# Seven block products for eight in the second half of a first MLP product, with a shorter weight conversion and Silu on ScalarE

## The chip, the cores and the metric

The kernel runs on one core of one Trainium2 chip. Its engines work side by side, each through a queue of its own in order: TensorE (PE in the profile; its weight loads are PEld), VectorE (DVE), ScalarE (ACT), GpSimd (POOL) and SyncE (SP), which here issues the transfers. They wait for one another by semaphores. The metric is device time in microseconds (us), as a median of several runs.

## The reference

Attention over 4 batches and 12 heads (448 tokens, 64 wide) with normed q and k feeds two MLP layers over 1792 tokens, 768 wide, hidden 2048:

```python
q_n, k_n = (rmsnorm(q, g_q), rmsnorm(k, g_k))
attn = softmax(scale * q_n @ k_n.T)                  # with the row's maximum taken off
x = (attn @ v) as 1792 x 768
h = x @ w_in;   x1 = (h * (1 / (1 + exp(-h)))) @ w_out        # first layer
h = x1 @ w2_in; r = maximum(h, 0); out = (r * r) @ w2_out     # second layer
```

The weights of both layers arrive as 64-bit floats; the kernel reads them as pairs of 32-bit words.

## The kernel before

**Numbers.** Each matmul operand is held in two parts: a high part (a cast to TensorE's 32-bit format) and a low part (the rest). A product is three matmuls: high x high, low x high, high x low. `split` makes the parts of activations, `parts` those of weights (`w_hi` by ScalarE or VectorE, `w_lo` by VectorE or GpSimd, L515 to L524).

**Weights.** `words` loads 64-bit weights into a buffer `raw` (a ring of three), and builds 32-bit floats from their words: an absolute value on ScalarE (L876), a clamp (L880), a shift (L884), the sign (L890) and the low bits (L896) on VectorE. It stores the result in device memory for later loads. The first layer's weights are converted in its first half (16 blocks of `w_in`, 24 of `w_out`); the 32 blocks of the second layer's weights are converted ahead of time, into a buffer `V`, during the first layer, by the list `BEFORE` and the function `ahead`.

**First layer.** Tokens lie in four batches of 448; the first half works on batches 0 and 1, the second on 2 and 3. A half has four quarters of four hidden blocks of 128. In a quarter, `up` makes, for each block and batch, 18 matmuls (six channel blocks by three) into a bank of the ring `t` (three banks), then a tanh on ScalarE (L989) and a multiply on VectorE (L994) give twice the Silu in `g`, which is split into `gg` (`g_hi`, `g_lo`). Then the out-projection goes into the ring `s` (four banks), and is added to `part` (L1043) with a factor 0.5; the last quarter's sums are stored as `y`.

**Second layer.** It treats its inputs as 2 x 2 blocks: two hidden blocks by two channel halves, and two channel halves by two batches. `combine` forms sums of input blocks (B11, T2, T3, T4, B21, T1, B22), `weights` sums of weight blocks (S1 to S4, L1161), and seven products (L1193, nine matmuls each) with sums out of the banks (`plus`, L1209, on VectorE) replace eight.

**Order.** The order on all engines is found when the program is built: `Plan` holds every step with a duration, runs them forward by due time, works the due times backward from the end, and keeps the best of several rounds. The attention's steps have fixed nominal times. Buffers come from rings, and a step that claims a buffer waits for the users of the one before.

## Time and profile before

| | us |
|---|---|
| median of three timed runs | 1199.5 |
| lowest and highest of them | 1197.34 and 1202.25 |
| the profiled execution | 1194.88 |
| its span | 1193.0 |

The page gives for each engine its busy time and share of the span: TensorE 98%, weight loads 88%, VectorE 77%, ScalarE 46%, GpSimd 21%. Attention fills the time up to about 272 us, the first layer the time to about 745 us, the second the rest. The granted clock of TensorE is full in all of the forty slices but no slice's transfers are: they move 185 GB/s on average.

### The profile page before, as it was taken

Reading aid. Unit: us, or ns where it says so; the run is one execution under the profiler, and the core shown is the slowest. Engines: PE = TensorE matmul, PEld = TensorE weight load, DVE = VectorE, ACT = ScalarE, POOL = GpSimd, SP = SyncE. Lnnn points to the kernel's source line nnn. Section 1 sums busy time; section 2 is a strip of 40 time slices with the busy share of each in tenths; the row PEclk is TensorE's granted clock in tenths of the full one; section 3 lists DMA queues with packets and bytes.
Section 4 is the critical chain, followed back from the end, with each engine's and each line's share of the span. In section 5 each row is a group of like instructions: output and inputs, shape, how many; then the busy total and the mean of one; then the engine's idle time right before and its main releaser. Section 6 shows DMA issues by size and latency. Waiting matters only on the chain.

```text
span 1193.0 us, 19008 instructions
## 1 busy us (share of the span) xinstructions
PE 1169.5 (98%) x6960; PEld 1047.8 (88%) x6960; DVE 921.9 (77%) x1610; ACT 543.3 (46%) x1140; POOL 245.1 (21%) x446
## 2 busy tenths in 40 slices
PE   5999999998999999999999999999999999999998
PEld 3777777777999999999999999899999999999998
DVE  7999999987999886878889868856677962555544
ACT  5999999973443233334433233433334433111111
POOL 3566666622000001111100001111112310000000
PEclk9999999999999999999999999999999999999999
DMA  6455447538666654878787738855557695444444
GB/s 169 87 82 88 91 87 115 87 56 196 215 192 208 180 160 136 314 252 267 224 249 232 252 128 299 322 199 199 199 199 265 236 355 188 147 146 146 146 164 128
DMA packets 134109, 220.75 MB, mean 185 GB/s; under 512 B 31104, under 2 KB 99456, under 8 KB 134016
## 3 DMA queue, kind: packets, MB, share of 16 engines
q1 hardware_dynamic: 134016, 219.54, 61.0%
q8 instruction: 55, 0.90, 0.3%
q14 instruction: 38, 0.31, 0.1%
HBM read 145.88 MB, written 73.62 MB: 184 GB/s over the span
## 4 chain that ended last, share of the span: by engine, by line
PE 94%; DVE 3%; DMA 2%; ACT 1%; SPq 0%; issue 0%; ACTq 0%
PE s L1269 20%; PE s L1031 18%; PE t L977 18%; PE t L1193 12%; PE t L704 7%; PE pv L753 6%; PE s L677 6%; PE pv L1193 5%; PE t L624 2%; DMA raw<-in_moe_w_out_dram 1%; DMA W<-kp 0%; DMA qk<-in_k_dram 0%; DVE W L896 0%; SPq L538 0%; DVE gg L524 0%
## 5 line engine op out<-in xcount | busy, mean ns | idle before, releaser
L977 PE MATMUL t<-xb,w 128*128 128x448 f32 x1152 | 240.3, 366 | 3.5 <-DVE g L994 3.5
L1031 PE MATMUL s<-gg,w 128*128 128x448 f32 x1152 | 240.2, 366 | 0.1
L977 PEld LDWEIGHTS t<-xb,w 128*128 128x128 f32 x1152 | 216.0, 188 | 22.8 <-DVE g L994 4.6
L1031 PEld LDWEIGHTS s<-gg,w 128*128 128x128 f32 x1152 | 216.1, 188 | 18.7 <-issue 0.4
L1269 PE MATMUL s<-w,gh 128*128 128x384 f32 x896 | 227.4, 334 | 0.0
L1269 PEld LDWEIGHTS s<-w,gh 128*128 128x128 f32 x896 | 162.1, 188 | 1.2
L1296 DVE TENSOR_TENSOR gg<-s,gg 128x384 f32<-128x384 f32 x196 | 107.6, 554 | 61.4 <-PE s L1269 61.1
L1269 PE MATMUL s<-w,gl 128*128 128x384 f32 x448 | 149.7, 334 | 0.0
L695 ACT ACTIVATE E<-s,mx 112x448 f32<-112x448 f32 x192 | 121.9, 646 | 20.9 <-ACT xf L503 13.0
L1209 DVE TENSOR_TENSOR g<-t,g 128x448 f32<-128x448 f32 x96 | 58.4, 620 | 80.5 <-ACT g L503 56.7
L688 DVE TENSOR_REDUCE mx<-s 112x1 f32<-112x448 f32 x192 | 107.3, 610 | 5.6 <-PE s L677 5.4
L704 PEld LDWEIGHTS t<-ident,E 112*112 112x112 f32 x768 | 73.8, 134 | 31.7 <-issue 14.9
L704 PE MATMUL t<-ident,E 112*112 112x112 f32 x768 | 95.1, 266 | 0.7 <-DVE T L640 0.4
L524 DVE TENSOR_TENSOR w<-W,w 128x768 fp32r<-128x768 f32 (+1 forms) x99 | 85.6, 872 | 3.6 <-ACT w L515 2.7
L1269 PEld LDWEIGHTS s<-w,gl 128*128 128x128 f32 x448 | 84.1, 188 | 0.0
L753 PE MATMUL pv<-PT,vv 112*64 112x224 f32 x768 | 83.0, 359 | 0.0
L515 ACT CAST w<-W 128x768 fp32r<-128x768 f32 (+1 forms) x61 | 45.1, 743 | 75.7 <-PE s L1031 48.9
L524 POOL TENSOR_TENSOR w<-W,w 128x512 fp32r<-128x512 f32 (+1 forms) x13 | 19.1, 1468 | 279.0 <-ACT w L515 219.5
L677 PE MATMUL s<-T 64*112 64x448 f32 x576 | 73.4, 384 | 1.8 <-ACT T L633 1.1
L1219 ACT ACTIVATE g<-g 128x448 f32<-128x448 f32 x48 | 27.5, 575 | 97.1 <-DVE g L1209 96.7
L524 POOL TENSOR_TENSOR gl<-g,gh 128x448 fp32r<-128x448 f32 x12 | 14.8, 1237 | 265.5 <-DVE gh L517 198.8
L753 PEld LDWEIGHTS pv<-PT,vv 112*64 112x64 f32 x768 | 51.1, 136 | 19.7
(112 smaller groups left out, 1772.4 us busy)
## 6 DMA issues: line engine op xcount, KB each, us to landing
raw<-in_moe_w_in_dram SPq DMA_DIRECT2D x32, 768.0 KB
raw<-in_moe_w_out_dram SPq DMA_DIRECT2D x24, 512.0 KB
raw<-in_moe_w_out_dram SPq DMA_DIRECT2D x16, 768.0 KB
su<-w SPq DMA_DIRECT2D x16, 768.0 KB
w<-su SPq DMA_DIRECT2D x16, 768.0 KB
xf<-y SPq DMA_DIRECT2D x48, 224.0 KB
ki<-W SPq DMA_DIRECT2D x16, 384.0 KB
ko<-W SPq DMA_DIRECT2D x24, 256.0 KB
```

The source lines that it names most:

```text
L524: kind, when, any_t(n, rate), lambda e: engine(e).tensor_tensor(o(), a(), h(), ALU.subtract),
L677: nc.tensor.matmul(pts[j].ap[:CP, :S], T.ap[r, 0, a, c * CP:(c + 1) * CP], T.ap[r, 1, b_], start=(k_ == 0), stop=(k_ == 2),)
L688: lambda e, pt=pt, mx=mx: nc.vector.tensor_reduce(mx.ap, pt.ap[:CP, :S], AX.X, ALU.max, negate=True),
L695: lambda e, j=j, c=c, pt=pt, mx=mx, E=E: nc.scalar.activation(E.ap[:, j], pt.ap[:CP, :S], AF.Exp, bias=mx.ap, accum_out=sums.ap[:, j, c:c ...
L704: nc.tensor.transpose(pe.ap[:CP, m * CP:(m + 1) * CP], E.ap[:, j, m * CP:(m + 1) * CP], ident.ap)
L753: nc.tensor.matmul(pv.ap[j * D:(j + 1) * D, c2 * CT * CP:(c2 + 1) * CT * CP], vr.ap[:, j * NCH + m, :], pt.ap[:, j * NCH + m].rearrange("p ...
L977: nc.tensor.matmul(pt.ap[:, :S], w_()[:, c, :], x[c // HC].ap[:, a, c % HC, :], start=(c == 0 and n == 0), stop=(c == NC6 - 1 and n == 2),)
L1031: nc.tensor.matmul(pt.ap[:, :S], w_()[:, f, :], gg.ap[:, k, a, f, :], start=(f == 0 and n == 0), stop=(f == HQ - 1 and n == 2),)
L1193: nc.tensor.matmul(pt.ap[:, :S], w_()[:, c0 + c, :], view(b, a, c)(), start=(start and c == 0 and k == 0), stop=(c == HC - 1 and k == 2), ...
L1209: lambda e: nc.vector.tensor_tensor(o.ap, pt.ap[:, :S], a.ap, ALU.add),
L1269: nc.tensor.matmul(pt.ap[:, :NH], g.ap[:, fi, tc_ * P:(tc_ + 1) * P], w_()[:, 0, nh * NH:(nh + 1) * NH], start=(n == 0), stop=(n == 5),)
L1296: lambda e, o=o, pt=pt: nc.vector.tensor_tensor(o(), pt.ap[:, :NH], o(), ALU.add),
```

## The change

- The second half of the first layer (`SEVEN = (1,)`) uses the scheme of the second layer: `first_x` forms its input blocks from the attention's results in device memory, two hidden blocks form a pair, and seven products of nine matmuls replace eight. `four` and `seven`, taken out of `layer2`, serve both layers. The weight sums S3 and S4 now overwrite W0 in place of a buffer V of their own.
- The Silu is one ScalarE instruction in place of a tanh and a multiply, so the factor 0.5 of the out-projection goes.
- The conversion of weights has a scale of 2^-112 in the absolute value, and no clamp.
- The second layer's weights are converted by another list `BEFORE`: 13 of the 32 from the first half's second quarter on, as the program lists them, by way of the buffers `gh` and `gl`, 19 in the second half.
- The planner runs eight rounds, and holds loads of `y`, of `first_x`'s blocks and of the second layer's 64-bit weights until 25 us ahead of their due time.

```diff
-BEFORE = list(range(40, 72))
+BEFORE = [int(12 + 2 * i) for i in range(13)] + [int(42 + 1.8 * i) for i in range(19)]
+SEVEN = (1,)
...
-ROUNDS = 6
+ROUNDS = 8
+AHEAD = 25.0
...
+        hold = [
+            end + d - AHEAD if end is not None and s.kind in ("load_raw2", "load_y") else 0.0 for s, d in zip(steps, due)
+        ]
...
+                    if st < hold[n]:
+                        st = hold[n]
...
-            raw = sb([P, 2 * UW], I32, "raw")
+            if tag == "V" and len(units) < len(SEGS) // 2 * (NFQ + NC6):
+                raw = sb([P, 2 * UW], I32, ("gh", "gl")[sum(k[0] in "pq" for k in kept) % 2], 1, "yp")
+            else:
+                raw = sb([P, 2 * UW], I32, "raw")
...
-                lambda e: nc.scalar.activation(f(), hi().bitcast(F32), AF.Abs), reads=[raw], writes=[W],
-            )
-            step(
-                "clamp" + nth, at, dve_t(m, 1920.0, True),
-                lambda e: nc.vector.tensor_scalar(f(), f(), C1, C2, ALU.max, ALU.min), writes=[W],
+                lambda e: nc.scalar.activation(f(), hi().bitcast(F32), AF.Abs, scale=SHIFTED), reads=[raw], writes=[W],
...
         step(
-            "tanh", at, {"act": (0.425, None, False)},
-            lambda e: nc.scalar.activation(g.ap, pt.ap[:, :S], AF.Tanh, scale=0.5),
-            reads=[pt], writes=[g],
-        )
-        step(
-            "silu", at, dve_t(S),
-            lambda e: nc.vector.scalar_tensor_tensor(g.ap, g.ap, 1.0, pt.ap[:, :S], ALU.add, ALU.mult),
+            "silu", at, {"act": (0.46, None, False)},
+            lambda e: nc.scalar.activation(g.ap, pt.ap[:, :S], AF.Silu),
             reads=[pt], writes=[g],
         )
...
+    def four(pair, at, keys):
...
+            two(S1, A21, A22, ALU.add, [W1], [Z])
+            two(S2, S1, A11, ALU.subtract, [W0], [Z])
...
+            for o, a in ((A11, A21), (A12, S2)):
+                step(
+                    "w_sum", at, any_t(W3), lambda e, o=o, a=a: engine(e).tensor_tensor(o(), o(), a(), ALU.subtract),
+                    reads=[W1 if a is A21 else Z], writes=[W0],
+                )
...
+    def seven(x, w, at, finish):
...
+        p1, p6, p7 = psum("pv"), psum("t"), psum("t")
+        u2, u3, c21, c11 = (sb([P, S], F32, "g") for _ in range(4))
+        product(p1, w0, 0, "B11")
+        copy_step("p1_copy", at, ("act", "dve"), lambda: u2.ap, lambda: p1.ap[:, :S], S, [p1], [u2])
+        product(p6, z, HC, "T2")
+        plus(u2, u2, p6)
+        product(p7, v_, 0, "T3")
+        plus(u3, u2, p7)
+        p4 = psum("t")
+        product(p4, a22, 0, "T4")
+        plus(c21, u3, p4)
+        finish(1, 0, c21)
+        product(p1, w0, HC, "B21", False)
+        finish(0, 0, c11, p1)
+        p5 = psum("t")
+        product(p5, z, 0, "T1")
+        plus(u3, u3, p5)
+        finish(1, 1, u3)
+        plus(u2, u2, p5)
+        p3 = psum("t")
+        product(p3, v_, HC, "B22")
+        plus(u2, u2, p3)
+        finish(0, 1, u2)
...
+        if h_ in SEVEN:
+            for f in range(0, NFQ, 2):
...
+                seven(xs[h_], four(pair, at, [f"i{k}{q_}_{f}" for k in "wazv"]), at, finish)
...
-                    return lambda e: nc.vector.scalar_tensor_tensor(
-                        o(), pt.ap[:, :S], 0.5, part.ap[:, e_, :], ALU.mult, ALU.add)
+                    return lambda e: nc.vector.tensor_tensor(o(), pt.ap[:, :S], part.ap[:, e_, :], ALU.add)
...
+    def first_x(half, early, late):
...
+        for c in range(HC):
+            b12, b22, b11 = (of(n, c, early) for n in ("B12", "B22", "B11"))
+            total(b22, b12, ALU.subtract, early)
+            put("T3", c, b22, early)
+            total(b11, b22, ALU.add, early)
+            put("T2", c, b11, early)
...
+        yield x
+        x["B11"] = [sb([P, HC, S], FR, tag, 1, "yp") for tag in ("gh", "gl")]
+        x.update({n: block() for n in ("B21", "T4", "T1", "B22")})
...
-    xs += [make_x(b) for b in range(2, B)]
+    blocks = first_x(1, ("seg", 1, 0.0), ("seg", NQ, 0.0))
+    xs = [xs, next(blocks)]
     for n in range(len(SEGS)):
+        if n == NQ:
+            next(blocks)
         layer1(n, xs)
```

On TensorE, the end of the second half's first quarter and the start of its second before (`t<-xb` is `up`, `s<-gg` the out-projection):

```order
L977 MATMUL t<-xb,w 128x448 x135
L1031 MATMUL s<-gg,w 128x448 x108
L977 MATMUL t<-xb,w 128x448 x9
L1031 MATMUL s<-gg,w 128x448 x18
L977 MATMUL t<-xb,w 128x448 x9
```

And now, the last products of a pair in that half and the out-projection behind them (L1075 is the seven-product, L1164 the out-projection):

```order
L1075 MATMUL t<-yb,w 128x448 x9
L1075 MATMUL t<-xb,v 128x448 x9
L1075 MATMUL pv<-xb,w 128x448 x9
L1075 MATMUL t<-xb,w 128x448 x9
L1164 MATMUL s<-gg,w 128x448 x6
L1075 MATMUL t<-xb,w 128x448 x9
L1164 MATMUL s<-gg,w 128x448 x108
```

The long runs of `up` have become runs of nine into the banks `t` and `pv` with inputs from several buffers; the out-projection keeps its place behind them.

On ScalarE, the start of the first layer before (L876 is the absolute value of a conversion, L989 the tanh):

```order
L876 ACTIVATE W<-raw 128x768
L989 ACTIVATE g<-t 128x448
L876 ACTIVATE W<-raw 128x768
L989 ACTIVATE g<-t 128x448
L515 CAST gg<-g 128x448
L876 ACTIVATE W<-raw 128x512
L989 ACTIVATE g<-t 128x448
```

And now (L887 the absolute value, L1000 the Silu, L523 a cast):

```order
L887 ACTIVATE W<-raw 128x768
L523 CAST w<-W 128x768
L1000 ACT_TABLE_LOAD
L1000 ACTIVATE g<-t 128x448
L887 ACTIVATE W<-raw 128x768
L1000 ACTIVATE g<-t 128x448
L523 CAST gg<-g 128x448
L887 ACTIVATE W<-raw 128x512
L1000 ACTIVATE g<-t 128x448
```

A weight cast and a table load stand ahead of the first Silu; the order behind it is the old one.

On SyncE's queue at the same place before (L869 loads 64-bit weights, L904 stores converted ones):

```order
L869 DMA raw<-in_moe_w_in_dram 128x6x256
L904 DMA ki_4592<-W 128x768
L869 DMA raw<-in_moe_w_out_dram 128x4x256
L904 DMA ki_4643<-W 128x768
L741 DMA R<-rd 64x448 x2
```

And now (L880 the loads, L911 the stores):

```order
L880 DMA raw<-in_moe_w_in_dram 128x6x256
L911 DMA ki_4590<-W 128x768
L880 DMA raw<-in_moe_w_out_dram 128x4x256
L911 DMA ki_4631<-W 128x768
L880 DMA gh<-in_moe_w_in_dram 128x6x256
L749 DMA R<-rd 64x448 x2
```

The first load of the second layer's weights (into `gh`) now stands right behind the first load of the first layer's `w_out`.

## Rows read from the trace of the kernel before

**Rows 1.** The page, busy time and share of each engine.
```profile
PE 1169.5 (98%) x6960; PEld 1047.8 (88%) x6960; DVE 921.9 (77%) x1610; ACT 543.3 (46%) x1140; POOL 245.1 (21%) x446
```

**Rows 2.** Waits of TensorE over the span: us, times, longest.
```profile
PE t L624 <- POOL y L603: 11.7, 1, 11.7
PE t L977 <- DVE g L994: 3.5, 1, 3.5
PE s L677 <- ACT T L633: 1.1, 1, 1.1
PE t L1193 <- ACT w L515: 1.0, 1, 1.0
PE s L677 <- DVE T L640: 0.7, 1, 0.7
PE t L704 <- DVE T L640: 0.4, 1, 0.4
PE t L704 <- ACT PT L503: 0.2, 1, 0.2
```

**Rows 3.** Stretches: length, each engine's busy us, granted clock, transfer engines' share, GB/s.
```profile
366.00:464.00 98.00, 98.00 (x485) 90.84 (x484) 82.08 (x135) 28.84 (x44) 1.29 (x1) 1.00 0.56 172
464.00:500.00 36.00, 35.97 (x175) 32.48 (x175) 33.75 (x61) 17.10 (x30) 7.11 (x4) 1.00 0.70 233
540.00:600.00 60.00, 60.00 (x298) 55.60 (x297) 50.14 (x76) 25.07 (x43) 6.72 (x5) 1.00 0.77 245
820.00:900.00 80.00, 80.00 (x427) 76.51 (x426) 54.74 (x94) 27.92 (x47) 11.27 (x9) 1.00 0.57 205
1100.00:1193.00 93.00, 88.49 (x475) 84.73 (x474) 46.18 (x85) 16.43 (x30) 3.48 (x3) 1.00 0.42 140
```

**Rows 4.** The chain that ended last: start us, length us, what.
```profile
337.51 27.36 PE t L977 x135
...
513.73 27.79 PE t L977 x135
...
806.10 1.85 PE t L1193 x9
```

**Rows 5.** The first layer's start, instructions in order of time; idle before in brackets.
```profile
279.95 0.55 ACT L989 ACTIVATE g<-t 128x448 f32<-128x448 f32 x1 [5.63 <-PE t L977]
...
289.03 0.66 ACT L876 ACTIVATE W<-raw 128x512 f32<-128x512 f32 x1 [1.66 <-DMA raw<-in_moe_w_out_dram]
289.60 0.53 ACT L989 ACTIVATE g<-t 128x448 f32<-128x448 f32 x1
...
292.68 0.61 DVE L994 SCALAR_TENSOR_TENSOR g<-g,t 128x448 f32<-128x448 f32 x1
...
293.34 6.96 PE L977 MATMUL t<-xb,w 128*128 128x448 f32 x33 [3.50 <-DVE g L994]
```

**Rows 6.** Groups by line and shape, ScalarE: busy us, mean ns | idle before.
```profile
L515 ACT CAST w<-W 128x768 fp32r<-128x768 f32 x35 | 29.3, 836 | 58.3 <-PE s L1031 37.6 <-PE s L1269 12.2 <-PE pv L1193 6.1
...
L549 ACT ACT_TABLE_LOAD x1 | 1.3, 1283 | 0.7 <-PEq L1349 0.7
```

**Rows 7.** The same view, VectorE.
```profile
L1209 DVE TENSOR_TENSOR g<-t,g 128x448 f32<-128x448 f32 x96 | 58.4, 620 | 80.5 <-ACT g L503 56.7 <-PE t L1193 21.9
...
L994 DVE SCALAR_TENSOR_TENSOR g<-g,t 128x448 f32<-128x448 f32 x64 | 39.0, 614 | 11.0 <-ACT g L989 10.8
...
L896 DVE SCALAR_TENSOR_TENSOR V<-raw,V 128x768 int32<-128x768 int32 x32 | 31.9, 998 | 0.5
L890 DVE SCALAR_TENSOR_TENSOR V<-raw,V 128x768 int32<-128x768 int32 x32 | 31.5, 984 | 0.6
...
L884 DVE TENSOR_SCALAR V<-V 128x768 int32<-128x768 int32 x32 | 18.8, 586 | 0.5
L880 DVE TENSOR_SCALAR V<-V 128x768 f32<-128x768 f32 x32 | 18.0, 561 | 16.6 <-ACT V L876 16.6
...
L880 DVE TENSOR_SCALAR W<-W 128x512 f32<-128x512 f32 x24 | 10.2, 423 | 3.4 <-ACT W L876 3.2
...
L1161 DVE TENSOR_TENSOR W<-W 128x384 f32<-128x384 f32 x13 | 7.5, 574 | 0.0
```

**Rows 8.** The same view, TensorE's weight loads of the first product.
```profile
L977 PEld LDWEIGHTS t<-xb,w 128*128 128x128 f32 x1152 | 216.0, 188 | 22.8 <-DVE g L994 4.6 <-issue 0.3
```

More of the change, by code (lines that the diff above doesn't have):

```diff
@@ L943, in first_in, with first_words @@
         return unit(w1_in[:, f * P:(f + 1) * P].rearrange("(c p) f -> p c f", p=P), NC6, P, at, f"i{f}")
+    def first_words(f, at):
+        ahead(at)
+        return words(w1_in[:, f * P:(f + 1) * P].rearrange("(c p) f -> p c f", p=P), NC6, P, at, f"i{f}")
     def first_out(f0, e, at):
@@ new lines, in seven, with product, products, plus @@
+    def seven(x, w, at, finish):
+        w0, a22, z, v_ = w
+        def product(pt, w, c0, n, start=True):
+            h, l, wh, wl = w
+            b = x[n]
+            def products(e):
+                for c in range(HC):
+                    for k, (w_, a) in enumerate(((wh, 0), (wl, 0), (wh, 1))):
+                        nc.tensor.matmul(
+                            pt.ap[:, :S], w_()[:, c0 + c, :], view(b, a, c)(),
+                            start=(start and c == 0 and k == 0), stop=(c == HC - 1 and k == 2),
+                            skip_group_check=True,
+                        )
+            step(
+                "prod", at, pe_t(PROD), products,
+                reads=[h, l] + [key(b, a, c) for a in range(2) for c in range(HC)], writes=[pt],
+            )
+        def plus(o, a, pt):
+            step(
+                "u_sum", at, dve_t(S),
+                lambda e: nc.vector.tensor_tensor(o.ap, pt.ap[:, :S], a.ap, ALU.add),
+                reads=[pt] + ([a] if a is not o else []), writes=[o],
+            )
+        p1, p6, p7 = psum("pv"), psum("t"), psum("t")
[21 more added lines that the diff above has]
+        finish(0, 1, u2)
@@ L1065, in layer1, with combine @@
                 )
-    def view(b, a, c):
-        return (lambda: b[a].ap[:, c, :]) if isinstance(b, list) else (lambda: b.ap[:, a, c, :])
-    def key(b, a, c):
-        return (b[a], c) if isinstance(b, list) else (b, (a, c))
-    def combine(half, at, later):
-        ya, yb = 2 * half, 2 * half + 1
-        if half:
-            x = {"B11": [sb([P, HC, S], FR, "raw") for _ in range(2)]}
-            x.update({n: block("yb", "yp") for n in ("T2", "T3")})
-            x.update({n: block() for n in ("T4", "B21", "T1")})
-        else:
-            x = {n: block("yb", "yp") for n in ("B11", "T2")}
-            x.update({n: block() for n in ("T3", "T4", "B21", "T1")})
-        x["B22"] = sb([P, 2, HC, S], FR, "part", None, "yp")
+    def combine(x, source, at, later):
         def chunk(c, at, names):
@@ L1133, in combine, with second_x @@
         return x
+    def second_x(half, at, later):
+        if half:
+            x = {"B11": [sb([P, HC, S], FR, "raw") for _ in range(2)]}
+            x.update({n: block("yb", "yp") for n in ("T2", "T3")})
+            x.update({n: block() for n in ("T4", "B21", "T1")})
+        else:
+            x = {n: block("yb", "yp") for n in ("B11", "T2")}
+            x.update({n: block() for n in ("T3", "T4", "B21", "T1")})
+        x["B22"] = sb([P, 2, HC, S], FR, "part", None, "yp")
+        return combine(x, lambda k, c: yk[2 * half + k, c], at, later)
@@ new lines, in first_x, with load, of, total @@
+    def first_x(half, early, late):
+        x = {n: block("yb", "yp") for n in ("T2", "T3")}
+        kept_t = {}
+        def load(d, at):
+            t = sb([P, S], F32, "xf")
+            step(
+                "load_y", at, dma_t(230), lambda e: engine(e).dma_start(t.ap, d.ap), reads=[d], writes=[t],
+            )
+            return t
+        def of(n, c, at):
+            return load(xk[2 * half + int(n[2]) - 1, (int(n[1]) - 1) * HC + c], at)
+        def total(o, a, op, at):
+            step(
+                "y_sum", at, any_t(S), lambda e: engine(e).tensor_tensor(o.ap, o.ap, a.ap, op), reads=[a], writes=[o],
+            )
+        def put(n, c, t, at):
+            split(
+                ("y_hi", "y_lo"), at, view(x[n], 0, c), view(x[n], 1, c), lambda: t.ap,
+                [t], [key(x[n], 0, c), key(x[n], 1, c)],
+            )
+        for c in range(HC):
+            b12, b22, b11 = (of(n, c, early) for n in ("B12", "B22", "B11"))
[3 more added lines that the diff above has]
+            put("T2", c, b11, early)
+            d = kept_t[c] = dram([P, S], f"t{half}_{c}", 1)
+            step(
+                "keep_t", early, dma_t(230), lambda e, d=d, t=b11: engine(e).dma_start(d.ap, t.ap),
+                reads=[b11], writes=[d],
+            )
+        yield x
+        x["B11"] = [sb([P, HC, S], FR, tag, 1, "yp") for tag in ("gh", "gl")]
+        x.update({n: block() for n in ("B21", "T4", "T1", "B22")})
+        for c in range(HC):
+            put("B11", c, of("B11", c, late), late)
+        for c in range(HC):
+            b21, t2 = of("B21", c, late), load(kept_t[c], late)
+            put("B21", c, b21, late)
+            total(b21, t2, ALU.subtract, late)
+            put("T4", c, b21, late)
+        for c in range(HC):
+            b12, b11 = of("B12", c, late), of("B11", c, late)
+            total(b12, b11, ALU.subtract, late)
+            put("T1", c, b12, late)
+        for c in range(HC):
+            put("B22", c, of("B22", c, late), late)
+        yield x
```

161 lines of the change are left out of this document (69 added, 92 removed).

## The prediction

> **What bounds the kernel now.** I read the page first. TensorE's matmuls cover 98% of the span and its weight loads 88% [rows 1]. The waits of TensorE come next: over the whole span it waits 18.6 us for another engine, of which 11.7 us is one wait in the attention's lead-in, 3.5 us one wait at the first layer's start, and 1.0 us one wait at the second layer's start [rows 2]. Between these it is never late: the table of stretches shows 60.00 of 60 us busy in the first layer and 80.00 of 80 in the second, at a granted clock of 1.00 throughout [rows 3]. So the time is the sum of TensorE's work plus a few waits, and the two questions are how much of that work goes and whether the other engines keep up. VectorE is the near one: 68% to 94% busy in those stretches, and in the fullest, 464 to 500 us, TensorE still ran 35.97 of 36 us [rows 3].
>
> **The product itself.** In the second half of the first layer, 16 blocks of hidden columns times two batches times 18 matmuls, 576, become eight pairs times seven products times nine, 504: 72 matmuls go. The chain of waits is work back to back, so it gives their price: 135 matmuls of the first product in 27.36 us [rows 4], 0.2027 us each. That is 14.6 us, all of it on the path.
>
> **The cadence.** The same chain shows two cadences at the same clock: the second layer's seven-products run nine in 1.85 us, 0.2056 each, and a stretch of the first layer ran 135 in 27.79 us, 0.2059 each [rows 4]. I don't know what selects it; its tiles are those of the neighbouring fast stretch. The 504 new matmuls have the form of the second layer's, so I take its cadence: 504 x 0.0029 = +1.5 us. Bounds: below, the second layer's 1008 products return to the fast cadence, -2.9, and the slow 135 of the first layer too, -0.4; above, all 2232 matmuls of the first layer run at 0.2059, 2232 x 0.0032 = +7.1.
>
> **The activation.** Before, a bank of the ring of three is freed by a tanh on ScalarE and then a multiply on VectorE. At 289.60 us the tanh of the bank that TensorE wants runs, but VectorE, in conversions, comes to the multiply only at 292.68, and TensorE starts again at 293.34 after 3.50 us [rows 5]. With one Silu on ScalarE that bank is free at about 290.15. What stands ahead of it there is what stood ahead of the tanh: a conversion that waits until 289.03 for its load [rows 5], which is issued from the same place in SyncE's queue as before. The rest of the wait is then about 0.5 us: -3.0 us. Bounds: -3.5 (none left) and 0 (a new activation-table load and one weight cast, which now stand ahead of the first Silu, delay all that follow). The table load took 1.28 us and a cast 0.84 [rows 6]; ScalarE was idle 5.63 us ahead of the first tanh [rows 5], so I take them as hidden. What is late next is the third product's input, the out-projection weights, now made behind one or two conversions for the second layer.
>
> The Trainium skill, ScalarE: Activation LUTs, "What ACT_TABLE_LOAD costs", puts 1.38 us of drain onto a load of 1.28, 2.66 in all. The trace has the 1.283 us, and no run shows the drain. By the page 0.84 + 2.66 = 3.50 still lies inside the idle 5.63, so the sum stays; the rule would bite if the table changed back and forth, and the order of ScalarE shows one such load more than before.
>
> **VectorE's work.** Gone: 72 clamps at 0.42 to 0.56 us and 64 multiplies at 0.614 us [rows 7], 76 us. Come: 48 sums out of PSUM at 0.620, 31 of the 32 new weight sums at 0.574 (one goes to GpSimd), and some 38 us for the larger set of weight and input splits, by the counts of the order. The evictions lose a factor of 0.5 and keep their shape: no price. The total grows by about 10 us, so the question is where it lies. For the second layer's weights, three steps of a conversion stay on VectorE, 0.586 + 0.984 + 0.998 = 2.57 us [rows 7]. By the order 28 of these conversions stood between the last eviction of the first half and that of the second; now 12 do. With the durations of such rows VectorE's instructions in that stretch add up to 208 us before and 189 after, while TensorE's work there shrinks by 13 of some 235. It has been 84% busy there [rows 3] and becomes no fuller.
>
> The first half takes the others. Its fullest part runs from the first eviction of its second quarter to the last of its third: 366 to 464 us, VectorE busy 82.08 of 98 [rows 3]. Out go 18 clamps (8.6) and 12 multiplies (7.4); in come seven conversions (18.0), two input sums with four splits (3.4), and the shift of some weight splits (about 6): +11. That makes 93 of 98 us, 95%, against the 94% of 464 to 500 us that cost TensorE nothing. I take 0, bounded by 0 below and one wait of the kind at the first layer's start above, 3.5 us.
>
> **New waits.** The trace has no first-layer stretch with seven-products, so the bounds come from the second layer and from the worst wait. Sixteen pairs of the second layer cost 1.04 us in one wait [rows 2]; eight pairs at that rate give 0.5. Two hand-overs are new: at the half's start the inputs T4, B21, T1 and B22 reuse the four buffers of the first half, and at the second layer's start T2 and B11 reuse buffers that the first layer now holds to its end. Both have 138 or more out-projection matmuls, 28 us, as cover, by the order; I give each 0.75 us, a little under the 1.04 of [rows 2]: +2.0 in all. Bounds: 0, and one 3.5 us wait in each of the four quarters, 14.0. The loads of these inputs are held back to 25 us ahead of their use as planned, and a block of 128 by 448 words, 0.23 MB, takes about 1 us at the 205 to 245 GB/s of [rows 3]: cover enough. The added transfers (input blocks reloaded, three kept sums) go through SyncE's queue in a stretch whose engines are 70% to 77% busy [rows 3]; ahead of a first-layer load stands at most one new load, so I give them no price of their own, and they are part of this upper bound.
>
> **Sum.** -14.6 + 1.5 - 3.0 + 2.0 = -14.1 us. The profiled execution took 1194.88 us (span 1193.0 and 1.9 around it) and becomes 1180.8. The three timed runs had a median of 1199.5, 4.6 above the profiled one; I carry that over: 1185.4, and forecast 1185.4 us. The end, where TensorE idles 4.5 us of the last 93 [rows 3], doesn't change.
>
> The Trainium skill, Perfetto Trace Analysis, "Identifying the Most-Contended Engine", holds matmul occupancy for a poor measure and judges TensorE by weight loads. By it TensorE has 12% of room here, and the change removes 72 x 0.188 us [rows 8] = 13.5 rather than 14.6, giving 1186.5. The trace bears out the matmul count: waits fill 19 us of the span, not 140, and the loads run beside matmuls that follow each other at 0.2027.
>
> **Rivals.**
> First, VectorE or a hand-over is late each quarter: the 14.0 us in place of 2.0, so 1197.4. For it: 95% full in one stretch, in-order queues, and a ring of three weight words that a pair fills whole. Against it: the second layer has the same rings and pattern and lost 1.04 us.
> Second, the slow cadence spreads over the first layer: +7.1 in place of 1.5, 1191.0. For it: the slow row holds for 135 matmuls on end, and lies in the half that changes. Against it: the fast row is as long, with the same tiles.
> Third, nothing new waits and the cadence turns fast where it was slow: 1185.4 - 2.0 - 1.5 - 3.3 = 1178.6.
> Fourth, slower: the sums out of PSUM come late. Each of the 48 frees one of three banks, and each may stand in VectorE's queue behind a 0.98 us conversion step; if every one costs TensorE half of that, 48 x 0.5 = 24 us, 1209.4. It cancels the gain at 0.29 us per sum and is slower by 0.5% from 0.42. For it: VectorE is 84% busy in the first layer, 68% in the second [rows 3]. Against it: there the same sums waited for TensorE or ScalarE for 80 us [rows 7], and three banks cover 3.7 us.
>
> **How the numbers follow.** About 0.5%, 6 us, is what a measurement of this kernel can tell from no change. Forecast (1180 to 1191): 0.60. First rival 0.13, second 0.12, third 0.10, fourth 0.05. Faster holds the forecast, the third, most of the second (0.11) and a quarter of the first (0.03): 0.84; same 0.11, slower 0.05. The range 1178 to 1196 leaves out the fourth, most of the first and the low side of the third.
>
> **What would show it.** Right: 504 matmuls of the seven-product in the first layer and 576 fewer of the old; the wait at 289.84 us down to about half a microsecond, with ScalarE as its releaser; TensorE 60 of 60 us in the stretches of the second half; waits of TensorE there under 3 us in all. Wrong: waits of the seven-product for VectorE's sums or for weight casts of several microseconds per quarter (first or fourth rival), or nine matmuls in 1.85 us and more through the first half (second).

## The result, and the profile after

Four runs of the changed kernel gave a median of 1183.35 us (1182.85 to 1184.83), against 1200.04 of the kernel before beside them (1197.34 to 1202.25): a ratio of 0.986, 95% interval 0.984 to 0.989. The forecast was 1185.4. The profiled execution took 1184.83, where the sum had put 1180.8 for it. Of all runs below only three of e8's twelve are slow ones, more than 1.5% above its lowest, and e8's numbers leave them out.

The page of the changed kernel, as [rows 1]:

```profile
PE 1156.8 (98%) x6888; PEld 1035.5 (88%) x6888; DVE 921.4 (78%) x1612; ACT 551.3 (47%) x1154; POOL 239.4 (20%) x445
```

72 matmuls are gone. VectorE's total is what it was; the sum had let it grow by about 10 us. Next the waits of TensorE over the span, as [rows 2] (us, times, longest):

```profile
PE t L632 <- POOL y L611: 11.4, 1, 11.4
PE t L1075 <- DMA w<-sz: 2.4, 1, 2.4
PE s L685 <- ACT T L641: 1.9, 1, 1.9
PE t L1075 <- DVE g L1090: 0.8, 1, 0.8
PE s L1367 <- DVE gl L532: 0.8, 2, 0.5
PE s L1367 <- DVE gg L1394: 0.7, 1, 0.7
PE s L1164 <- DVE gg L532: 0.7, 1, 0.7
PE s L685 <- DVE T L648: 0.7, 1, 0.7
PE t L988 <- ACT g L1000: 0.7, 1, 0.7
```

L988 is the old first product, L1075 the seven-product of both layers, L1164 the first layer's out-projection, L1367 the second layer's. The 3.5 us wait of the first layer's start has become the 0.7 of the last row, but four rows of the second layer (w<-sz, g, gl and L1394's gg) have come for the one of 1.0 that it had, and one of the out-projection (L1164). The stretches, with the columns of [rows 3], show where:

```profile
366.00:464.00 98.00, 98.00 (x485) 90.84 (x484) 90.24 (x141) 34.44 (x50) 4.85 (x4) 1.00 0.88 282
464.00:500.00 36.00, 36.00 (x180) 33.37 (x179) 34.94 (x64) 17.92 (x33) 2.58 (x2) 1.00 0.71 227
540.00:600.00 60.00, 60.00 (x298) 55.62 (x297) 37.50 (x65) 18.82 (x33) 2.87 (x2) 1.00 0.31 96
820.00:900.00 80.00, 79.68 (x426) 75.90 (x425) 64.77 (x109) 28.62 (x49) 20.05 (x16) 1.00 0.70 255
900.00:1000.00 100.00, 96.42 (x499) 90.62 (x498) 59.35 (x111) 39.31 (x74) 14.85 (x9) 0.98 0.70 242
```

In these stretches of the first layer TensorE is never late, not even at 366 to 464 us, where VectorE now has 90 of 98 us busy. The largest loss lies at 900 to 1000 us, where the second layer changes halves. The first layer's start, in order of time, against [rows 5]:

```profile
278.69 1.28 ACT L1000 ACT_TABLE_LOAD   x1
280.46 0.55 ACT L1000 ACTIVATE g<-t 128x448 f32<-128x448 f32 x1 [0.48 <-PE t L988]
...
290.41 0.53 ACT L1000 ACTIVATE g<-t 128x448 f32<-128x448 f32 x1
...
290.99 9.19 PE L988 MATMUL t<-xb,w 128*128 128x448 f32 x44 [0.66 <-ACT g L1000]
```

The bank is freed by ScalarE at 290.94 and TensorE goes on at 290.99. The table load ends at 279.97, before TensorE has anything for the Silu at 280.46: it is hidden. (In e4 below the first Silu waits for nothing else and starts 0.02 us behind the load's end; the load takes 1.28 us there too.)

**An account of both layers.** The start times of the matmuls can be read from the trace, and their intervals, from one start to the next, give three numbers for a kernel: the time from the first layer's first matmul to the last of all; the lost time, which is the sum over intervals longer than 0.26 us of what they have above 0.203; and the mean of the other intervals in each half of the first layer, here called the cadence. All are from one profiled execution each.

| | profiled, us | both layers, us | lost, us | cadence, first layer's halves, ns |
|---|---|---|---|---|
| before | 1194.88 | 915.3 | 6.4 | 203.6, 202.9 |
| changed | 1184.83 | 904.5 | 10.9 | 202.9, 202.7 |
| e1, eight products | 1201.27 | 921.1 | 13.1 | 202.7, 202.7 |
| e2, a product twice | 1205.78 | 924.6 | 11.1 | 203.2, 206.7 |
| e3, before with light conversion and Silu | 1205.53 | 923.3 | 7.2 | 206.4, 206.4 |
| e4, clamp and tanh back | 1195.28 | 915.1 | 20.7 | 203.8, 202.7 |
| e5, changed again | 1184.24 | 904.5 | 10.6 | 202.9, 202.7 |
| e6, sums planned for VectorE | 1185.18 | 904.8 | 7.0 | 202.9, 206.5 |
| e7, no hold | 1214.25 | 934.6 | 40.9 | 202.7, 202.9 |
| e8, a second queue | 1200.86 | 920.4 | 26.0 | 202.7, 202.7 |
| e9, sums in place on VectorE | 1190.86 | 907.4 | 5.9 | 206.1, 206.7 |
| e10, clamp back | 1190.16 | 905.0 | 11.4 | 202.7, 202.7 |
| e11, only raw weights held | 1186.09 | 901.8 | 8.0 | 202.8, 202.9 |
| e12, e9 once more | 1179.06 | 899.2 | 5.9 | 202.9, 202.7 |

From before to changed: 72 x 0.2027 = 14.6 off, 4.5 more lost, and 1.1 off by the cadence (269 matmuls of the first layer, 55 us, that ran at 206.7 ns run at 202.7 now) make -11.2, and the table has -10.8. Some 0.3 of the difference is the account's own: ten of the added intervals stand in the second layer's out-projection, where one is otherwise 0.174 us and not 0.203. The lost time fell from 5.1 to 2.5 us in the first layer and grew from 1.3 to 8.4 in the second.

The attention is not in this account, and it varies: the first layer's first matmul comes at 272.6 to 275.4 us of the span in eleven of the traces, but at 276.2, 278.2 and 277.5 in e9, e10 and e11, which were run together.

### The profile page after: what moved, and what is told of

It reads as the page before. It is cut to its first block, busy times and chain, and to the rows that moved or that the text cites. A ratio compares the mean times of both kernels' runs of the same rounds, so it can differ in the third digit from the quotient of the medians.

```text
span 1183.0 us, 18930 instructions
## 1 busy us (share of the span) xinstructions
PE 1156.8 (98%) x6888; PEld 1035.5 (88%) x6888; DVE 921.4 (78%) x1612; ACT 551.3 (47%) x1154; POOL 239.4 (20%) x445
## 4 chain that ended last, share of the span: by engine, by line
PE 91%; DVE 5%; DMA 3%; issue 1%; SPq 0%; ACT 0%; DVEq 0%; ACTq 0%
PE s L1164 19%; PE s L1367 18%; PE t L1075 18%; PE t L988 7%; PE t L712 7%; PE pv L1075 7%; PE pv L761 6%; PE s L685 6%; PE t L632 2%; DMA raw<-in_moe_w_in_dram 1%; DMA w<-sz 1%; DVE w L532 1%; DMA qk<-in_k_dram 0%; DVE g L1090 0%; DVE W L903 0%
## 5 line engine op out<-in xcount | busy, mean ns | idle before, releaser
L1164 PE MATMUL s<-gg,w 128*128 128x448 f32 x1152 | 238.8, 365 | 0.8 <-DVE gg L532 0.7
L1164 PEld LDWEIGHTS s<-gg,w 128*128 128x128 f32 x1152 | 216.2, 188 | 18.8 <-DVE gg L532 1.4
L1367 PE MATMUL s<-w,gh 128*128 128x384 f32 x896 | 227.7, 334 | 0.7 <-DVE gg L1394 0.7
L1367 PEld LDWEIGHTS s<-w,gh 128*128 128x128 f32 x896 | 162.3, 188 | 2.2 <-DVE gg L1394 1.1
L1090 DVE TENSOR_TENSOR g<-t,g 128x448 f32<-128x448 f32 x144 | 87.3, 620 | 93.1 <-ACT g L511 53.9
L1394 DVE TENSOR_TENSOR gg<-s,gg 128x384 f32<-128x384 f32 x196 | 107.0, 554 | 57.0 <-PE s L1367 56.6
L1367 PE MATMUL s<-w,gl 128*128 128x384 f32 x448 | 150.0, 335 | 0.9 <-DVE gl L532 0.8
L988 PE MATMUL t<-xb,w 128*128 128x448 f32 x576 | 119.2, 366 | 0.7 <-ACT g L1000 0.7
L988 PEld LDWEIGHTS t<-xb,w 128*128 128x128 f32 x576 | 108.0, 188 | 10.2 <-ACT g L1000 1.0
L523 ACT CAST w<-W 128x768 fp32r<-128x768 f32 (+1 forms) x73 | 54.5, 750 | 125.4 <-PE s L1164 46.5
L532 DVE TENSOR_TENSOR w<-W,w 128x768 fp32r<-128x768 f32 (+1 forms) x121 | 107.3, 896 | 6.8 <-ACT w L523 5.9
L712 PEld LDWEIGHTS t<-ident,E 112*112 112x112 f32 x768 | 73.8, 134 | 32.0 <-issue 14.6
L1367 PEld LDWEIGHTS s<-w,gl 128*128 128x128 f32 x448 | 84.1, 188 | 1.9 <-DVE gl L532 1.9
L1075 PE MATMUL t<-yb,w 128*128 128x448 f32 x360 | 80.2, 372 | 2.4 <-DMA w<-sz 2.4
L1075 PE MATMUL t<-xb,w 128*128 128x448 f32 x360 | 79.9, 367 | 0.0
L511 ACT COPY g<-pv 128x448 f32<-128x448 f32 x24 | 12.7, 531 | 140.1 <-PE pv L1075 130.6
L1075 PEld LDWEIGHTS t<-yb,w 128*128 128x128 f32 x360 | 68.5, 191 | 8.5 <-DMA w<-sz 2.7
```

The lines of the kernel that those rows point to most:

```text
L532: kind, when, any_t(n, rate), lambda e: engine(e).tensor_tensor(o(), a(), h(), ALU.subtract),
L712: nc.tensor.transpose(pe.ap[:CP, m * CP:(m + 1) * CP], E.ap[:, j, m * CP:(m + 1) * CP], ident.ap)
L988: nc.tensor.matmul(pt.ap[:, :S], w_()[:, c, :], x[c // HC].ap[:, a, c % HC, :], start=(c == 0 and n == 0), stop=(c == NC6 - 1 and n == 2),)
L1075: nc.tensor.matmul(pt.ap[:, :S], w_()[:, c0 + c, :], view(b, a, c)(), start=(start and c == 0 and k == 0), stop=(c == HC - 1 and k == 2), ...
L1090: lambda e: nc.vector.tensor_tensor(o.ap, pt.ap[:, :S], a.ap, ALU.add),
L1164: nc.tensor.matmul(pt.ap[:, :S], w_()[:, f, :], gg.ap[:, k, a, f, :], start=(f == 0 and n == 0), stop=(f == HQ - 1 and n == 2),)
```

## The experiments

A change of a step's engine or duration makes the planner order the whole program anew, so most of these kernels differ from the changed one in more than the edit; e9 and e12 do not, and e5 is the changed kernel itself. Ratios are to the kernel before on the same chip, with 95% intervals; its medians there were 1198.99 (e1 to e4), 1199.64 (e5 to e8), 1204.23 (e9 to e11) and 1197.62 (e12).

**e1: eight products.**

```diff
-SEVEN = (1,)
+SEVEN = ()
...
-    blocks = first_x(1, ("seg", 1, 0.0), ("seg", NQ, 0.0))
-    xs = [xs, next(blocks)]
+    xs = [xs, [make_x(b) for b in range(2, B)]]
```

> The changed kernel with eight products for seven in the second half of the first layer; Silu, the lighter conversion, the list BEFORE, eight planner rounds and the hold stay. Theory (the count of matmuls carries the gain): 72 matmuls come back at 0.2027 us, +14.6 on 1183.4, so 1198.0, and against the kernel before only the 2.8 us of the first-layer-start wait remain, 1197. Rival (the relief of VectorE carries it, the seven products are only its occasion): within 3 us of the changed kernel, 1183 to 1186.

1200.82 us, ratio 1.0024 (0.9997 to 1.0050). The count of matmuls carries the gain; all that stays of the change, without the seven products, shows no gain. In the account both layers are 16.6 us longer than in the changed kernel: 14.6 and 2.2 of lost time, less some 0.3 by the cadence.

**e2: a product twice.**

```diff
         product(p3, v_, HC, "B22")
+        if at[0] == "seg":
+            product(p3, v_, HC, "B22")
```

> The changed kernel with the seventh product of each of the eight first-layer pairs done twice into the same bank (the second overwrites the first): 72 matmuls more, no work more on any other engine. Theory (TensorE sets the time, every matmul is on the path): +14.6, 1198.0, with the second half of the first layer at 100% busy as before. Rival (another engine or the transfers set the pace there and the matmuls only fill the time): less than half of it, under 1190.5.

1203.08 us, ratio 1.0025 (1.0001 to 1.0048): the theory's sign, 5 us more than its size. The account gives 20.1 us: 14.6 for the matmuls, 0.2 lost, 4.9 because the second half ran at 206.7 ns (1152 x 4.0 ns = 4.6, and 0.3 in the first), and some 0.3 in the second layer's cadence. The lowest of its ten runs, 1197.05, is 14.2 above the lowest of the changed kernel.

**e3: the kernel before with the Silu and the light conversion.**

```diff
-                "clamp" + nth, at, dve_t(m, 1920.0, True),
...
-            lambda e: nc.scalar.activation(g.ap, pt.ap[:, :S], AF.Tanh, scale=0.5),
...
+            lambda e: nc.scalar.activation(g.ap, pt.ap[:, :S], AF.Silu),
```

> The kernel before with the Silu on ScalarE and without the clamp (the lighter conversion), nothing else of the change. Theory (VectorE was covered, only one wait goes): the 3.5 us wait at the first layer's start becomes about 0.7, so 1200.0 - 2.8 = 1197.2. Rival (VectorE's load cost TensorE time in many places): 8 us or more faster, under 1192. Third possibility: the wait only moves, 1200.

1199.86 us, ratio 1.0001 (0.9966 to 1.0036): neither the theory nor its rival, but the third possibility. The wait at the start fell (3.87 us between two matmuls before, 1.22 and 0.76 at two places now), but its trace has 2.0 us of `t <- DVE g` and 1.5 of `s <- DVE gl` at the second layer that before had not, so the lost time is 7.2 for 6.4: the wait moved. What shows more is the spread: the ten runs lie at 1193.97 to 1196.76 and at 1202.95 to 1207.11, and nothing between, so that the median is a time that no run had. The profiled one, of the upper group, ran the first layer at 206.7 ns from a wait of 0.78 us that ends at 311 us to 739 us, shortly before its end, at a clock of 1.00:

```profile
366.00:464.00 98.00, 98.00 (x476) 89.02 (x475) 69.43 (x109) 27.51 (x41) 0.00 (x0) 1.00 0.55 164
```

TensorE is as busy as in [rows 3], but it does 476 matmuls where it did 485. Over 2304 matmuls 4.0 ns are 9.2 us; the groups are 10 apart. No run of the lower group has a trace, so that the groups are the two cadences is likely and not shown.

**e4: clamp, tanh and multiply back in the changed kernel** (the multiply in the first half, the clamp everywhere).

```diff
+                "clamp" + nth, at, dve_t(m, 1920.0, True),
...
-            lambda e: nc.scalar.activation(g.ap, pt.ap[:, :S], AF.Silu),
+            lambda e: nc.scalar.activation(g.ap, pt.ap[:, :S], AF.Tanh, scale=0.5),
```

> The changed kernel with the clamp back in every conversion and the tanh and multiply back in the first half; seven products and all else stay. Theory (the relief is not needed, only the first-layer-start wait comes back): +2.8, 1186.2. Rival (the relief makes the room for the conversions moved to the first half): VectorE has 90.2 of 98 us busy at 366 to 464 us now; 18 clamps and 12 multiplies add 8.6 + 7.4 us, 106 of 98, so 8 us of TensorE waits there and the 2.8 beside them, 1194 or more.

1196.86 us, ratio 0.9971 (0.9952 to 0.9990): the rival by the time, and by its reason in part. Waits, then stretches:

```profile
PE t L632 <- POOL y L611: 11.8, 1, 11.8
PE t L992 <- DVE g L1009: 3.4, 1, 3.4
PE t L1084 <- DMA w<-sz: 2.9, 1, 2.9
PE t L992 <- DVE w L532: 2.3, 3, 0.9
```

```profile
294.00:298.00 4.00, 4.00 (x12) 3.52 (x12) 4.00 (x7) 2.10 (x4) 1.39 (x1) 0.50 0.60 214
366.00:464.00 98.00, 96.86 (x474) 88.30 (x473) 95.90 (x159) 37.67 (x59) 14.11 (x10) 1.00 0.79 251
```

VectorE is at 95.90 of 98 us and TensorE waits there, 1.1 us, for the two parts of a weight. The old wait at the start is back, and this time the granted clock fell behind it, to 0.50, the 1.2 GHz level: 13 matmuls at 0.373 us and one at 0.541 are 2.6 us more. The same wait in the kernel before had no such fall. So over half of the 9.8 us that are lost beyond the changed kernel's is the multiply's wait (2.7 us longer than the Silu's) with its clock. The rest is for the most part waits for VectorE in the first layer (`w` 2.3 us, `g` 0.7, `part` 0.6), which is what the rival had in mind. That the relief makes the room for the moved conversions is thus shown for these few us alone.

**e10: the clamp alone back.**

```diff
+                "clamp" + nth, at, dve_t(m, 1920.0, True),
```

> The changed kernel with the clamp back in every conversion; Silu on ScalarE and all else stay. With clamp, tanh and multiply back the first layer's first half was 9.8 us longer, VectorE 95.90 of 98 us busy at 366 to 464. Theory (VectorE's room decides, each part by its size there): the clamp is 8.6 of the 16 us, VectorE at about 98.8 of 98 if nothing moves, so 3 to 7 us of TensorE waits in the first half, 1188 to 1192. Rival (the tanh and multiply alone, which hold the banks, did it): 1185 to 1187.

1193.52 us, ratio 0.9901 (0.9867 to 0.9934). The time is in the theory's range, but its mechanism is not there:

```profile
366.00:464.00 98.00, 98.00 (x486) 90.83 (x485) 96.52 (x161) 40.14 (x60) 2.82 (x2) 1.00 0.81 265
```

VectorE at 96.52 of 98 us costs TensorE nothing here. The first half lost 4.6 us for the 2.5 of the changed kernel, and both layers together lost 0.5 more. Of the 5.3 us that this profile is above the changed kernel's, 4.9 are the attention ahead of the first layer (278.2 us for 273.3), and the kernel before was itself at 1204 in that comparison. The clamp by itself is worth 2 us at most in the account; the rival is nearer.

**e5: the changed kernel again.**

> The changed kernel itself, unaltered, for the spread of its runs. The traces so far show two cadences of a first-layer matmul at a full clock, 202.7 and 206.7 ns, and a flip between them only at a wait of TensorE; the ten runs of the kernel before with only the Silu and the lighter conversion lie in two groups, 1194 to 1197 and 1203 to 1207. Theory (each execution draws its cadence at its waits): the changed kernel has slow runs too, up to 2232 x 0.004 = 8.9 us above the fast ones, so runs from 1183 to 1192 and a median of 1184 to 1188. Rival (the first four runs are its nature: its long stretch without a wait always runs fast): all runs between 1182 and 1186, median 1183.4.

1185.34 us (1184.24 to 1187.02 in six runs), ratio 0.9880 (0.9862 to 0.9899). Nearer the rival: no run near 1192, and the profiled first layer is at 202.7 ns from 291 us on, as in the first profile; but two runs pass its 1186, and the median lies in the theory's 1184 to 1188. The other sentence of the expectation, that the cadence changes only at waits, falls with e2, e4 and e6: there it went from 202.7 to 206.7 in the middle of an out-projection or a product, behind no interval longer than 0.21 us. And e9 below shows that a quick first layer is not this program's nature either.

**e6: the second layer's input sums planned for VectorE.** First the place, in the changed kernel: SyncE's issues, a sum on GpSimd, and TensorE, in order of time.

```profile
913.50 15.83 SPq L1208 DMA_DIRECT2D xf<-y  x11
929.58 0.32 SPq L927 DMA_DIRECT2D v<-sa  x1
930.74 5.37 POOL L1216 TENSOR_TENSOR xf<-xf 128x448 f32<-128x448 f32 x1 [14.11 <-DMA xf<-y]
936.14 1.27 SPq L1208 DMA_DIRECT2D xf<-y  x3
937.50 0.38 SPq L927 DMA_DIRECT2D w<-sw  x1
...
938.92 0.64 SPq L927 DMA_DIRECT2D w<-sz  x1
...
950.75 3.50 PE L1075 MATMUL t<-yb,w 128*128 128x448 f32 x9 [2.41 <-DMA w<-sz]
```

The sum on GpSimd, 1.15 us in two others of this stretch, takes 5.37 and ends at 936.11; SyncE's next load goes out 0.03 us later, and the weights `sz`, for which TensorE waits at 948 us, are behind it in the queue. Nine matmuls then take 3.50 us for 1.85, near the 1.2 GHz level (columns of [rows 3]):

```profile
951.00:954.00 3.00, 3.00 (x9) 2.69 (x10) 0.00 (x0) 0.77 (x2) 0.15 (x1) 0.53 1.03 402
```

The same link stood in the kernel before. What SyncE's queue waited for at this place, first in the changed kernel (925 to 940 us), then in the kernel before (940 to 960 us):

```profile
SPq L1208 <- POOL xf L1216: 5.5, 1, 5.5
```

```profile
SPq L1097 <- POOL xf L1105: 4.2, 1, 4.2
```

And the place in the kernel before, in order of time:

```profile
948.31 4.42 POOL L1105 TENSOR_TENSOR xf<-xf 128x448 f32<-128x448 f32 x1 [1.40 <-DMA xf<-y]
952.76 0.32 SPq L1097 DMA_DIRECT2D xf<-y  x1
953.17 0.38 SPq L920 DMA_DIRECT2D w<-sw  x1
...
954.08 0.42 SPq L920 DMA_DIRECT2D w<-sz  x1
...
962.48 2.02 PE L1193 MATMUL t<-yb,w 128*128 128x448 f32 x9
```

There `sz` went out 8.4 us ahead of its product and came in time; in the changed kernel 11.8 us passed from its issue to its product, 2.4 of them as a wait. What differs is the order of the queue: one load of an input block was left behind the sum in the kernel before, three are in the changed kernel, and they go out ahead of `sz`. Six of the 14 traces have a sum of more than 4 us here. The two with one load left behind it (before, e3) have no wait for `sz`; the four with two (e4) or three (changed, e2, e5) have one of 2.4 to 2.9 us. That these loads are what delays `sz` fits all six, but was not tried by itself.

```diff
-                    "y_sum", at, any_t(S), lambda e: engine(e).tensor_tensor(o.ap, a.ap, b.ap, op),
+                    "y_sum", at, dve_t(S), lambda e: engine(e).tensor_tensor(o.ap, a.ap, b.ap, op),
```

> The changed kernel with the second layer's sums of input blocks (31 in all, a few of them on GpSimd) kept on VectorE. At 930.74 us of the changed kernel one such sum took 5.37 us on GpSimd; SyncE's next load waits for the buffer it frees and starts at 936.14, and the weight loads sw and sz queued behind it at 937.50 and 938.92. Theory (this link makes the wait of the second layer's half change): the loads go out 4 to 5 us earlier, the wait of some 3.6 us there goes, 1183.4 - 3.6 = 1179.8. Rival (the transfers themselves or the ring of weights set that time, GpSimd's sum only happens beside it): the wait stays within 1 us, 1183.

1184.26 us (1180.72 to 1189.47), ratio 0.9867 (0.9843 to 0.9891). The mechanism held and the time did not move: the lost time fell by 4.0 us (6.2 less in the second layer, 2.2 more in the first, whose order is new), TensorE was busy 99.97 of 100 us at 900 to 1000, and the second half of the first layer ran at 206.5 ns, 1080 x 3.8 = 4.1 us back.

**e9 and e12: the same sums on VectorE, but in their old place.** The planner plans as before; the sums of the second layer's second half that it puts on GpSimd are issued on VectorE in the place that they had in the order. By the traces these are six; a seventh on GpSimd, in the first half, stays there.

```diff
+                    "y_sum", at, any_t(S),
+                    lambda e: (nc.vector if second else engine(e)).tensor_tensor(o.ap, a.ap, b.ap, op),
```

> The changed kernel with the seven GpSimd sums of the second layer's second half put on VectorE in the same place of the order; the order of all else is kept, so that the first layer is the same program. Earlier, with all such sums planned for VectorE, the wait at the half change went (stall of that half 4.2 to 0.2 us) but the first layer, ordered anew, drew the slow cadence from 505 us on, and the median stayed. Theory (one slow sum on GpSimd holds SyncE's queue and makes the wait): 4 us less than the 1185.3 of the changed kernel beside it, 1181.3, with the first layer at 202.7 ns throughout. Rival (on VectorE the sum waits for its load and holds that queue instead): 1184 to 1188.

> The same program as in the run with the seven sums in place on VectorE, once more. There the first layer, instruction for instruction that of the changed kernel, ran at 206.7 ns a matmul from the wait at 323 us on, where the changed kernel twice ran at 202.7 from that same wait, and its six runs lay between 1180.92 and 1197.27. Theory (the cadence is drawn anew at each wait in each execution): the runs spread over about 10 us again, with the low ones at 1180 to 1182, about 3 us under the changed kernel's lowest 1182.85; a profiled run at the fast cadence has a first layer of 455 us, at the slow one of 463. Rival (the program or its place in memory fixes the cadence): the profiled run is slow again, 463 us, and no run is under 1184 but by accident; median 1188 to 1192.

e9: 1189.40 us (1180.92 to 1197.27), ratio 0.9865 (0.9825 to 0.9904). e12, the same program: 1178.28 us (1177.37 to 1186.17), ratio 0.9839 (0.9807 to 0.9870). (The 323 us of the expectation, as e9's 505, count from the trace's first record, some 11 us ahead of the span's start.) In both the wait for `sz` is gone, and one for `gl` grew from 0.5 to 1.2 us; SyncE's queue in e12, against the changed kernel's above:

```profile
912.02 15.83 SPq L1208 DMA_DIRECT2D xf<-y  x11
928.10 0.32 SPq L927 DMA_DIRECT2D v<-sa  x1
929.53 1.69 SPq L1208 DMA_DIRECT2D xf<-y  x3
932.04 0.32 SPq L927 DMA_DIRECT2D w<-sw  x1
...
934.06 1.13 SPq L927 DMA_DIRECT2D w<-sz  x1
```

The three loads follow `v<-sa` after 1.4 us, not 6.6. Lost time falls from 10.9 to 5.9 us in both executions. But their first layers differ, first e9's, then e12's:

```profile
600.00:660.00 60.00, 60.00 (x292) 54.49 (x291) 50.97 (x83) 23.59 (x37) 4.19 (x3) 1.00 0.60 198
```

```profile
600.00:660.00 60.00, 60.00 (x298) 55.60 (x297) 51.80 (x82) 23.61 (x38) 5.73 (x4) 1.00 0.59 200
```

One program on one chip, fully busy at a clock of 1.00, with 292 matmuls in 60 us in one execution and 298 in the other. Their first layers take 463.3 and 455.3 us; the attention before them differs by another 3.6. So e9's rival (the queue held by VectorE) is out, and of e12's that the program fixes the cadence; its other half, the place in memory, was not recorded. At the quick cadence this is the best version of the study: its profile is 5.8 us under the changed kernel's first and 5.2 under its second, and the lost time accounts for 5.0 and 4.7 of it. The two ratios together, 0.9865 and 0.9839, do not part it from the changed kernel's 0.9863 and 0.9880.

**e7: no hold on the loads; e11: the hold for raw weights only.**

```diff
-AHEAD = 25.0
+AHEAD = 1e6
```

```diff
-            end + d - AHEAD if end is not None and s.kind in ("load_raw2", "load_y") else 0.0 for s, d in zip(steps, due)
+            end + d - AHEAD if end is not None and s.kind == "load_raw2" else 0.0 for s, d in zip(steps, due)
```

> The changed kernel without the hold on loads (AHEAD so large that no load is held). Theory (the hold does not make the wait of the second layer's half change: in both programs SyncE's queue has the same loads in the same order there): the wait stays at 3 to 5 us and the time at 1183 to 1185. Rival (the hold delays the loads of y and so makes that wait): it goes, 1179.8. Third: unheld loads of second-layer weights and input blocks crowd the first half's, and TensorE waits there, 1188 or more.

> The changed kernel with the hold on loads of the second layer's 64-bit weights only; loads of y and of the first layer's input blocks are free. Without any hold the first half lost 31 us in waits for casts and conversions on VectorE and ScalarE. Theory (unheld conversions come too early into VectorE's and ScalarE's queues and stand ahead of the first layer's own casts): holding them alone is enough, 1184 to 1187. Rival (the early loads of input blocks take the buffers xf and the queue): 1205 or more.

e7: 1220.56 us, ratio 1.0166 (1.0139 to 1.0192), the third possibility, far beyond its 1188. Waits, and the worst stretch:

```profile
PE t L988 <- DVE w L525: 9.3, 2, 5.8
PE s L1164 <- ACT w L523: 7.9, 2, 6.4
```

```profile
300.00:366.00 66.00, 50.23 (x217) 43.62 (x216) 50.77 (x81) 23.55 (x39) 1.17 (x1) 0.87 0.90 306
```

TensorE waits for the casts of the first layer's own weights; VectorE and ScalarE, which make them, are not full (50.77 and 23.55 of 66 us), but wait in their order for one another and for loads. e11: 1186.62 us, ratio 0.9839 (0.9810 to 0.9869), 8.0 us lost: its theory. Holding the raw weights is enough. What in the unheld order makes the waits was not taken apart further. Neither e7 nor e11 waits for `sz`, so e7's theory, that this wait stays, did not hold. But neither has a GpSimd sum of more than 2.4 us at that place, so they don't show whether the hold on the loads of `y` has a part in the wait; e9 and e12 lose it with the hold in force.

**e8: a second queue for the second layer's weights.**

```diff
-                "load_parts" + nth, at, dma_t(m), lambda
+                "load_parts" + nth, at, dma_t(m, 300.0, ("sp", "act") if nth else ("sp",)), lambda
```

> The changed kernel with the planner free to issue the second layer's loads of split weights from ScalarE's queue as well as SyncE's. Theory (a load queued behind loads of input blocks that wait for buffers makes the wait): a load of weights on another queue goes out when its own buffer is free, the wait shrinks by 2 us or more, 1180 to 1181.5. Rival (the buffer or the transfer is late, not the queue): no gain at that place, 1183, or a loss of 1 to 3 us where ScalarE's work waits behind an issue.

1203.08 us (1192.40 to 1209.53), ratio 1.0027 (0.9998 to 1.0056). Worse than either:

```profile
PE s L1367 <- DMA w<-su: 13.4, 6, 4.1
```

The second half of the second layer lost 18.6 us, most of it in six waits for the out-projection's weights. An issue on ScalarE stands in the order of ScalarE's own work; how far that is the cause here was not tried.

## Why the prediction was right, and where it was not

**The product: right.** 14.6 us for 72 matmuls, all on the path. e1 and e2 put the matmuls back in two ways and got it back, and the account closes with it.

**The cadence: wrong sign, and the idea behind it wrong.** The sum gave the seven-products the second layer's cadence, +1.5. The whole second half ran at 202.7 ns, and the slow stretch of [rows 4] did too: -1.1. The two cadences don't belong to a kind of product: the seven-products of the first layer ran at 202.7 ns here and at 206.7 in e9. Those of the second layer, which the sum took as its model, have a mean of 205.8 to 206.2 in all 14 traces, also behind a quick first layer; why is open. A first layer holds one cadence for up to 440 us. It comes back to 202.7 mostly behind an interval over 0.22 us, a wait or a remnant of one, but in e3, at 739 us, in the middle of an out-projection with no such interval; it falls to 206.7 behind a wait (e3, e9) or in the middle of work (e2, e4, e6).

**The activation: right, with a limit.** 3.50 became 0.66 with ScalarE as releaser, -2.8 for -3.0. But e3 shows that the wait can come back elsewhere, and in the changed kernel another wait of the out-projection's start, 0.7 us for `gg`, came behind it: the first half's lost time fell by 1.8 us, from 4.3 to 2.5.

**VectorE: right.** 90 of 98 us for the 93 forecast, at no cost. Its total did not grow by the 10 us of the working (921.4 for 921.9), which had no price in the sum. e4 shows the edge, which is not the busy share alone: at 95.90 TensorE waited 1.1 us for weight parts, at 96.52 (e10) not at all.

**New waits: the step that failed.** The sum had 2.0 us, for the eight pairs and two hand-overs that the change adds. The eight pairs and the half's start cost nothing (no interval over 0.26 us from the half's start to the second layer's), the second layer's start little more than before (1.8 us for 1.3). The waits came in the second layer, which the prediction took as unchanged: 5.9 us are lost where its halves change (937 to 954 us), and with the sums there on VectorE 1.4 are left (e12). A sum on GpSimd holds SyncE's queue there, as it did in the kernel before; the new order left more loads behind it. Lost time grew by 4.5 us; the sum had it fall by 1.0. And the hold on loads had no term at all, only "cover enough": without it the program as the planner then orders it loses 30 us more.

**The carry-over: wrong.** The 4.6 us between the profiled execution before and its median were added to the sum. The profile before, 1194.88, was a low one: 31 runs of that kernel on one chip reach from 1194.35 to 1206.19. The cadence is the likely reason (all but 72 us of that profile's first layer ran at 202.7 ns), but no second profile of that kernel shows it. The changed kernel's ten runs lie at 1182.85 to 1187.02, its two profiles at the quick cadence but for the first 80 matmuls. Other stretches, the attention for one, vary as well: e9 reached the first layer 3.6 us later than e12. So the profile went from 1194.88 to 1184.83, -10.1 for -14.1, and the median by -16.7. The profile came out 4.0 above the sum: 5.5 more lost than the sum had, 2.6 less by the cadence, and 1.1 from the rest. The median lies 1.5 under the profile, where 4.6 above it were carried over, 6.1 the other way. That these cancel to 2.1 is luck.

**The rivals.** The first (VectorE late each quarter) and the fourth (sums out of PSUM) did not come: no wait for the seven-product's sums in the first layer. The second (the slow cadence spreads) is real as a draw of an execution: e9 is it. The third, nothing new waiting and the quick cadence everywhere, came in no run. e12, with the wait for `sz` taken out, has 1178.28 for its 1178.6, but with 5.9 us lost and the second layer's seven-products at 205.9 ns, so that this is luck too.

## What to carry to other kernels

Before a profile's time is carried over to a median, count the matmuls per microsecond in it: a full engine at a full clock can still run at another rate in another execution. Where a planner orders everything anew, look for new waits in the parts that the change does not name, at each place where a queue of loads waits for a buffer that another engine frees; an edit with the order held, as in e9, shows such a link by itself. And a nearly full VectorE costs nothing until what it makes or frees is what TensorE wants next: a bank or the parts of a weight.

## What the runs showed of the hardware that was not expected

- Two rates of the same matmul, 202.7 and 206.7 ns for 128x448, at a granted clock of 1.00. The one is left for the other behind a wait or without one, and then held for tens or hundreds of us. Over a first layer of 2232 matmuls the difference is 8.9 us. What decides it stays open: e9 and e12 are the same program on the same chip.
- A wait of TensorE cost more than itself in some kernels and not in another. Behind the 3.4 us of e4 the granted clock fell to 0.50, behind the 2.4 us of the changed kernel, at 951 us, to 0.53. In the kernel before, with 3.5 us, it was full over the wait and what follows:

```profile
290.00:300.00 10.00, 6.66 (x33) 6.19 (x34) 9.72 (x16) 3.75 (x8) 2.59 (x2) 1.00 0.59 184
```

  In e4 and in the kernel before TensorE had been in the first product ahead of the wait. The length of the wait alone does not decide; what does is open.
- A GpSimd sum of 128x448 took 4.4 to 5.4 us at the second layer's half change in six traces (5.37 in the changed kernel), where two others of the changed kernel in that stretch took 1.15. In all six VectorE ran splits and casts beside it without a pause; but beside sums of 1.15 us it is often busy throughout as well. The runs don't show what makes the difference.
